# Moving a mixed block to third place and a whole product to the end: the late stage of an attention and MLP-mixer kernel

## The chip, the cores and the metric

The kernel runs on one core of one Trainium2 chip. A core has several engines that run at the same time, each through its own list of instructions in order: TensorE (PE) multiplies matrices into PSUM banks, VectorE (DVE), ScalarE (ACT) and GpSimd (POOL) work element by element, SyncE (SP) issues transfers (DMAs). An engine waits on semaphores that others raise. The metric is device time in microseconds (us) of one execution; three runs of the kernel before gave 1227.75, 1227.9 and 1229.17, median 1227.9.

## The reference

The inputs are q, k, v of shape (8, 8, 576, 64) (batch, head, token, feature), a scalar tau, and four weights. All is float32.

```python
scores = scale * np.matmul(q, k.transpose(0, 1, 3, 2))
thresh = np.max(scores, axis=-1, keepdims=True) - tau
scores = np.where(scores >= thresh, scores, -1000000000.0)
attn = softmax(scores)                       # written out in the reference
x = np.matmul(attn, v)                       # then (B,H,S,D) -> (B, S, H*D)
h = np.maximum(x^T @ w_tok1, 0.0) @ w_tok2   # over tokens, 576 -> 256 -> 576
u = x + h^T
h2 = np.maximum(u @ w_ch1, 0.0) @ w_ch2      # over channels, 512 -> 1536 -> 512
return u + h2
```

The last two lines are what this document is about: for each of the 8 x 576 tokens, u has 512 channels, the hidden layer 1536.

## The kernel before

**The planner.** The kernel is a Python program that writes out the instruction lists. For most of the work it makes operations (`sched.op`) with an engine, an assumed cost, the operations they depend on and a rank; a list scheduler then walks a clock of assumed times and emits them one after another, so that each engine's order is fixed when the program is built. Semaphore waits follow from the data, not from the assumed times. An operation on TensorE that needs a PSUM bank is made by `put_bank`, one that goes on in the same bank by `put_more`; `put_mid` reads a bank, and `put_leave` reads it and gives it back.

**The early stage** (to about 864 us) does attention batch by batch, the token products, and the channel products of a part of the tokens. What is put off: of batches 1 to 6 the second 256 tokens, of batch 7 all, and of every batch the last 64 tokens (576 is 256 + 256 + 64). Put-off values of batches 0 to 6 lie in DRAM (`spill`), those of batch 7 in SBUF (`xTs[7]`).

**The late stage** takes what was put off in five blocks of 512 tokens (class `Late`; the list is `groups`, made at L1377 to L1381). Before, they are: batches 1 and 2, batches 3 and 4, batches 5 and 6, batch 7's first 512 tokens, and last the "rests", 64 tokens from each of the 8 batches. A block's values are loaded into one of two buffers `u` (`load`, one DMA per batch; L1447 in the profile); batch 7's own block needs no load. The output rows are stored in four quarters of 128 rows (`store`, L1455), one DMA per batch in the quarter: a block of two batches, or of batch 7, has four stores of 128 rows, the rests have eight of 64 rows.

**A block.** Channels and tokens are each cut into two halves of 256, and a product of 2 x 2 such blocks is made with seven products in place of eight (Strassen's method in Winograd's form), with sums and differences on VectorE. `make_first` does the first layer in six rounds. Meanwhile VectorE transposes u in 32 x 32 blocks (`turn_u`, L1483, into `us`), and 16 DMAs per block bring the pieces into place (`move_u`, L1490, from `us` to `ut`), since the output is token by channel and has u added to it.

**The second layer** (`make_second`) is done for two halves m = 0, 1, each with 128 + 128 tokens (t = 0, 1) and 256 + 256 channels (n = 0, 1). Write o(t, n) for a piece of the output in `us` and old(t, n) for the same piece of u in `ut`. Three of its seven products, x1, x2 and x5, are whole ones (`plain`, six matrix multiplications of 128 x 256). The other four, x4, x6, x7 and x3, are split again into seven small products each of three multiplications of 128 x 128 (`make_inner`, called with 0 to 3). The whole product x5 is of `sum_place(0, m)` with `w2s[:, 0]`; it belongs into o(1, 1) and o(0, 1). Before, `y5b` adds it to old(0, 1) and `y5` puts it with old(1, 1) into o(1, 1). The last steps are sums: `q00`, `q01a`, `q01b`, `u2`, `u3`, `q10a`, `q10b`, `q11`, on POOL or VectorE as the planner finds; of these `q11` adds `w7` (which then holds u3) to o(1, 1), and `q01b` adds u2 (`w6_place`) to o(0, 1). The stores follow: the quarter t = 1 needs `q10b` and `q11`, the quarter t = 0 needs `q00` and `q01b`.

In the profile all late products have the line L1430 (`multiply`), all sums L946 (`add`) and differences L949 (`sub`), so they are told apart by tile names: `ga` and `hidden_b` hold the hidden layer, `x_sb`, `late_a` and `late_x` lend their space for sums, `small_a` and parts of the former two hold the small products' intermediate sums, `w` stands for several weights and for `w7`.

Of the kernel before, what the change touches and what calls it, by code (L numbers as in the profile page):

```python
# [21 lines left out]
def kernel(  # L22
# [25 lines left out]
    nc = tc.nc  # L48
    B, H, S, D = q.shape
# [15 lines left out]
    GR = 2 * P  # L65
# [29 lines left out]
    HJ, HD = NJ // 2, DM // 2  # L95
    w2s = const.tile([P, 3, HJ, HD], F32, name="w2s")
# [630 lines left out]
    sched = Scheduler()  # L727
# [217 lines left out]
    def add(out, a, b, eng=None):  # L945
        (eng or nc.vector).tensor_tensor(out=out, in0=a, in1=b, op=ALU.add)  # L946

    def sub(out, a, b, eng=None):
        (eng or nc.vector).tensor_tensor(out=out, in0=a, in1=b, op=ALU.subtract)  # L949
# [390 lines left out]
    def home(what):  # L1340
        if what not in homes:
            homes["g"] = work.tile([P, HJ, 2 * GR], F32, tag="g", bufs=1, name="ga")
            homes["a"] = work.tile([P, NTK, DM], F32, tag="a", bufs=1, name="late_a").rearrange("p m x -> p (m x)")
            homes["xT"] = work.tile([P, NP, S], F32, tag="xT", name="late_x").rearrange("p c x -> p (c x)")
        return homes[what]
# [4 lines left out]
    def sum_place(kind, m):  # L1350
        i = 2 * kind + m
        at = flat[:, TILE * i : TILE * i + TILE] if i < 3 else home("a")[:, 0:TILE]
        return at.rearrange("p (j x) -> p j x", x=P)
# [23 lines left out]
    REST = S - 2 * GR  # L1377
    put_off = [(b, GR * i, GR) for b in range(B) for i in range(NOW[b], 2)]
    groups = [put_off[i : i + 2] for i in range(0, len(put_off), 2)]
    assert all(len(g) == 2 for g in groups) and not NOW[B - 1]  # L1380
    groups.append([(b, 2 * GR, REST) for b in range(B)])  # L1381

    pending = [x for x in sched.ops if x.end is None and x.row is not None]
    last = [x for x in pending if x.row < B - 1]
# [27 lines left out]
    def put_bank(cost, work, deps, rank):  # L1412
        x = sched.op("pe", cost, work, deps, rank)
        x.bank = True
        return x
# [4 lines left out]
    def put_mid(on, cost, fn, x, deps, rank=1):  # L1420
        return sched.op(on, cost, lambda: fn(x.bank[1]), deps, rank)

    def put_leave(on, cost, fn, x, deps, rank=1):
        y = sched.op(on, cost, fn, deps, rank)
        y.frees = x
        return y

    def multiply(to, pairs, start=True):
        for x, (l, r) in enumerate(pairs):
            nc.tensor.matmul(to, lhsT=l, rhs=r, start=start and x == 0, stop=x == len(pairs) - 1, skip_group_check=not start)  # L1430

    small_used = [[], []]

    class Late:
# [12 lines left out]
                nc.sync.dma_start(out=self.u[:, :, at : at + n], in_=src)  # L1447
                at += n

        def store(self, t, rows):  # L1450
            at = 0
            for b, lo, n in groups[self.n]:
                first, last = max(at, P * t), min(at + n, P * t + P)
                if first < last:
                    nc.sync.dma_start(  # L1455
                        out=out[b, lo + first - at : lo + last - at, :], in_=rows[first - P * t : last - P * t]
                    )
                at += n
# [115 lines left out]
        def make_second(self, hidden, moved):  # L1574

            def a(i, k, m):
                return (hidden_b if k else home("g"))[:, :, GR * i + P * m : GR * i + P * m + P]

            def o(t, n, m):
                return self.us[m][:, t].rearrange("q a x -> q (a x)")[:, HD * n : HD * n + HD]  # L1580

            def old(t, n, m):
                return self.ut[m][:, t].rearrange("q k (c d) -> q c k d", c=NCC)[:, HC * n : HC * n + HC]

            def four(x):
                return x[:, 0:HD].rearrange("q (c k d) -> q c k d", c=HC, k=4)

            self.second, self.stores, self.outs = [], [[], []], [[], []]
            past_sums = list(self.past_second)
            h11, h12, h2 = hidden["11"], hidden["12"], hidden["2"]  # L1590

            def plain(l, r, deps):
                x = put_bank(2.57, lambda bank: multiply(bank[:, 0:HD], [(l()[:, j, :], r()[:, j, :]) for j in range(HJ)]), deps, 3.6 + 2 * self.n)
                self.second.append(x)
                return x

            def on_pool(fn, deps, rank=3):
                return sched.op("pool", 0.85, lambda: fn(nc.gpsimd), deps, rank, other=("dve", 0.36, lambda: fn(nc.vector)))

            s1, s2, s3, s4, y2, x2 = ([None, None] for _ in range(6))  # L1600
            for m in range(2):
                s1[m] = sched.op("dve", 0.96, lambda m=m: add(sum_place(0, m), a(1, 0, m), a(1, 1, m)), h12 + h2 + past_sums, 2)
            for m in range(2):
                s2[m] = sched.op("dve", 0.96, lambda m=m: sub(sum_place(1, m), sum_place(0, m), a(0, 0, m)), [s1[m]] + h11 + past_sums, 2)
                s3[m] = sched.op("dve", 0.96, lambda m=m: sub(a(1, 0, m), a(0, 0, m), a(1, 0, m)), [s1[m]] + h11, 2)
            c1, y5, y5b = [None, None], [None, None], [None, None]
            x1 = []
            for m in range(2):
                x2[m] = plain(lambda m=m: a(0, 1, m), lambda: side2(1, 0), h2)
                y2[m] = put_leave("dve", 0.42, lambda bank, m=m: add(four(o(0, 0, m)), four(bank), old(0, 0, m)), x2[m], [x2[m]] + moved[m])  # L1610
                x1.append(plain(lambda m=m: a(0, 0, m), lambda: side2(0, 0), h11))
                c1[m] = put_leave("act", 0.37, lambda bank, m=m: nc.scalar.copy(out=p1_place(m), in_=bank[:, 0:HD]), x1[m], [x1[m]] + past_sums, 0)
                s4[m] = sched.op("dve", 0.96, lambda m=m: sub(a(0, 1, m), a(0, 1, m), sum_place(1, m)), [s2[m], x2[m]], 2)
            for m in range(2):
                x5 = plain(lambda m=m: sum_place(0, m), lambda: w2s[:, 0], [s1[m]])
                y5b[m] = put_mid("dve", 0.42, lambda bank, m=m: add(old(0, 1, m), four(bank), old(0, 1, m)), x5, [x5] + moved[m])
                y5[m] = put_leave("dve", 0.42, lambda bank, m=m: add(four(o(1, 1, m)), four(bank), old(1, 1, m)), x5, [x5, y5b[m]] + moved[m])
            w7_of = lambda m: w7[:, m, :]
            w4 = self.make_inner(0, lambda m: a(1, 1, m), lambda m: o(1, 0, m), [h2, h2], s1, [moved[0], moved[1]])
            w6 = self.make_inner(1, lambda m: sum_place(1, m), w6_place, [[s2[0]], [s2[1]]], s4, [past_sums, past_sums])  # L1620
            w7s = self.make_inner(2, lambda m: a(1, 0, m), w7_of, [[s3[0]], [s3[1]]], [], [past_sums, past_sums])
            w3 = self.make_inner(3, lambda m: a(0, 1, m), lambda m: o(0, 1, m), [[s4[0]], [s4[1]]], x2, [moved[0], moved[1]])
            all_second = []
            for m in range(2):
                q00 = on_pool(lambda eng, m=m: add(o(0, 0, m), o(0, 0, m), p1_place(m), eng), [y2[m], c1[m]])
                u2 = on_pool(lambda eng, m=m: add(w6_place(m), w6_place(m), p1_place(m), eng), w6[m] + [c1[m]], rank=2)
                q01a = on_pool(lambda eng, m=m: add(four(o(0, 1, m)), four(o(0, 1, m)), old(0, 1, m), eng), w3[m] + [y5b[m]])
                q01b = on_pool(lambda eng, m=m: add(o(0, 1, m), o(0, 1, m), w6_place(m), eng), [q01a, u2])
                u3 = on_pool(lambda eng, m=m: add(w7_of(m), w7_of(m), w6_place(m), eng), w7s[m] + [u2], rank=2)
                q10a = on_pool(lambda eng, m=m: add(four(o(1, 0, m)), four(o(1, 0, m)), old(1, 0, m), eng), w4[m])  # L1630
                q10b = on_pool(lambda eng, m=m: add(o(1, 0, m), o(1, 0, m), w7_of(m), eng), [q10a, u3])
                q11 = on_pool(lambda eng, m=m: add(o(1, 1, m), o(1, 1, m), w7_of(m), eng), [y5[m], u3])
                self.outs[m] = [q00, q01b, q10b, q11]
                for t, deps in ((1, [q10b, q11]), (0, [q00, q01b])):
                    count = 2 if len(groups[self.n]) > 2 else 1
                    self.stores[m].append(
                        sched.op("sp", 0.6, lambda m=m, t=t: self.store(2 * t + m, self.us[m][:, t].rearrange("q a x -> q (a x)")), deps, 1, dmas=(count, 256 // count, 0.6))
                    )
                all_second += self.outs[m]
            self.past_next = all_second + self.second  # L1640

# [95 lines left out]
```

## Time and profile before

| what | us |
|---|---|
| median of three runs | 1227.9 |
| the profiled execution's own time | 1229.42 |
| its span, first to last instruction | 1227.6 |
| first stores of the five late blocks issued at | 938.74, 1009.29, 1079.85, 1150.42, 1218.01 |
| TensorE's last product begins and ends | 1219.02, 1219.93 |
| last instruction on VectorE ends | 1222.26 |
| mean granted TensorE clock | 0.997 |

In the profile, a row of a timeline gives start, length, engine, line, operation, "output<-inputs", shape, the number of merged instructions and, in brackets, the idle time before it and who ended it. SPq is SyncE's queue of transfers. One multiplication of this float32 kernel is two rows on TensorE. Rows of TensorE overlap, so the pitch from start to start says more than the length. PEld is the load of weights beside the products.

### The profile page before, as it was taken

To read this page: it belongs to the slowest core of one execution; us is meant where nothing else is said; L and a number is where in the kernel's file an instruction comes from. 1 tells how busy PE (TensorE), PEld (TensorE's weight loads), DVE (VectorE), ACT (ScalarE), POOL (GpSimd) and SP (SyncE) were. 2 spreads that over 40 slices of the span, in tenths; PEclk is the share of its full clock that TensorE was granted. 3 is DMA by queue.
4 is the path that set the end of the run, shared out by engine and by line. 5 is a ranking of instruction groups with operands and counts; after the bars stand their busy time and mean duration, and the time that the engine had idled before them with its cause. 6 is when DMAs were issued, how large, how long until landed. Compare 5 with 4: busy or idle time off the path is not lost.

```text
span 1227.6 us, 21546 instructions
## 1 busy us (share of the span) xinstructions
PE 1199.0 (98%) x7769; PEld 972.6 (79%) x7769; DVE 877.8 (71%) x1406; ACT 572.6 (47%) x1279; POOL 365.7 (30%) x568
## 2 busy tenths in 40 slices
PE   9888999999999999999999999999999999999996
PEld 8655788777777777876877777788899898999986
DVE  6798996777778668776867766843767575766756
ACT  6987863555663665574555456530211212121220
POOL 3666552333343423332433323411001010110101
PEclk9999999999999999999999999999999999999999
DMA  8656867767778757877767687661211202020101
GB/s 145 140 121 163 234 169 169 153 145 179 175 161 185 174 124 178 182 158 168 161 153 168 151 183 152 151 165 34 52 35 47 58 18 53 1 69 1 54 17 35
DMA packets 325370, 149.76 MB, mean 122 GB/s; under 512 B 223824, under 2 KB 318032, under 8 KB 325264
## 3 DMA queue, kind: packets, MB, share of 16 engines
q1 hardware_dynamic: 323392, 148.17, 52.9%
q8 instruction: 62, 1.02, 0.3%
q10 hardware_dynamic: 1872, 0.21, 0.1%
q14 instruction: 44, 0.36, 0.1%
HBM read 47.32 MB, written 13.50 MB: 50 GB/s over the span
## 4 chain that ended last, share of the span: by engine, by line
PE 85%; DVE 2%; DMA 0%; ACT 0%; issue 0%; SPq 0%; DVEq 0%
PE bank L1430 28%; PE bank L1058 12%; PE bank L982 11%; PE sc L848 10%; PE bank L371 8%; PE bank L460 5%; PE bank L478 5%; PE bank L366 3%; PE bank L1073 2%; DVE mx L865 1%; PE bank L441 0%; DVE us L946 0%; DVE g L1066 0%; DMA lk<-in_k_dram 0%; ACT e L881 0%
## 5 line engine op out<-in xcount | busy, mean ns | idle before, releaser
L881 ACT ACTIVATE e<-sc,bias 128x576 f32<-128x576 f32 x288 | 194.3, 742 | 173.1 <-POOL bias L871 171.9
L286 POOL TENSOR_SCALAR e<-e,rr 128x576 f32<-128x576 f32 x288 | 216.6, 769 | 189.3 <-DVE rr L278 187.8
L891 ACT ACTIVATE e<-e,ntau 128x576 f32<-128x576 f32 x288 | 220.8, 780 | 0.2
L865 DVE TENSOR_REDUCE mx<-sc 128x2 f32<-128x1152 f32 x144 | 188.1, 1348 | 40.5 <-PE sc L848 39.8
L316 DVE STREAM_TRANSPOSE T<-e 128x1152 f32<-128x1152 f32 x126 | 171.0, 1365 | 31.0 <-POOL e L286 21.8
L1058 PE MATMUL bank<-xT,wc 128*128 128x256 f32 x768 | 177.1, 383 | 1.9 <-ACT g L1063 0.9
L848 PE MATMUL sc<-kT,qT 64*128 64x192 f32 (+1 forms) x1920 | 165.5, 333 | 1.0 <-ACT e L881 1.0
L1058 PEld LDWEIGHTS bank<-xT,wc 128*128 128x128 f32 x768 | 143.0, 190 | 28.9 <-issue 4.4
L848 PEld LDWEIGHTS sc<-kT,qT 64*128 64x128 f32 (+1 forms) x1920 | 138.4, 176 | 31.2 <-issue 19.3
L371 PE MATMUL bank<-eT,lv 128*64 128x384 f32 (+1 forms) x1024 | 135.1, 406 | 0.0
L371 PEld LDWEIGHTS bank<-eT,lv 128*64 128x64 f32 x1024 | 73.7, 137 | 50.5 <-issue 44.3
L871 POOL TENSOR_SCALAR bias<-mx,toff 128x2 f32<-128x2 f32 x144 | 39.3, 273 | 193.1 <-DVE mx L865 186.0
L946 POOL TENSOR_TENSOR us<-us,late_x 128x256 f32<-128x256 f32 x14 | 13.1, 934 | 219.9 <-DVE us L946 156.9
L982 PE MATMUL bank<-wc,g 128*128 128x256 f32 x336 | 77.8, 381 | 0.0
L478 PE MATMUL bank<-w,a 128*128 128x192 f32 (+1 forms) x256 | 74.4, 425 | 1.2 <-DVE xT L489 0.7
L460 PE MATMUL bank<-x_sb,w 128*128 128x256 f32 x320 | 73.0, 383 | 0.7 <-DVE x_sb L445 0.5
L982 PEld LDWEIGHTS bank<-wc,g 128*128 128x128 f32 x336 | 63.1, 190 | 12.8 <-issue 2.5
L460 PEld LDWEIGHTS bank<-x_sb,w 128*128 128x128 f32 x320 | 59.8, 190 | 10.9 <-issue 1.1
L478 PEld LDWEIGHTS bank<-w,a 128*128 128x128 f32 x256 | 43.6, 192 | 22.5 <-issue 6.4
L1430 PE MATMUL bank<-t,w1s 128*128 128x256 f32 x240 | 60.8, 379 | 0.0
L946 DVE TENSOR_TENSOR temps<-bank,temps 128x256 f32<-128x256 f32 x60 | 25.3, 422 | 49.5 <-PE bank L1430 47.1
L1430 PE MATMUL bank<-t,wc 128*128 128x256 f32 x240 | 59.2, 379 | 0.0
(175 smaller groups left out, 1820.0 us busy)
## 6 DMA issues: line engine op xcount, KB each, us to landing
eT<-T SPq DMA_DIRECT2D x504, 144.0 KB, 3.0
w2s<-in_moe_w_ch_dram SPq DMA_DIRECT2D x24, 512.0 KB, 4.2
lk<-in_k_dram SPq DMA_DIRECT2D x122, 72.0 KB, 2.9
ut<-us SPq DMA_DIRECT2D x136, 64.0 KB, 2.1
lq<-in_q_dram SPq DMA_DIRECT2D x120, 72.0 KB, 3.1
out_dram<-us SPq DMA_DIRECT2D x32, 256.0 KB, 2.1
lv<-in_v_dram SPq DMA_DIRECT2D x112, 72.0 KB, 2.5
spill<-xT SPq DMA_DIRECT2D x6, 640.0 KB, 4.0
```

Of the source, the lines that this page charges most:

```text
L286: nc.gpsimd.tensor_scalar(out=eh, in0=eh, scalar1=rr[:, h : h + 1], scalar2=1.0, op0=ALU.mult, op1=ALU.mult)
L316: nc.vector.transpose(out=T.rearrange("p a (c x) -> p c a x", c=NK), in_=e.rearrange("p (c a x) -> p c a x", c=NK, a=4))
L371: nc.tensor.matmul(to[r], lhsT=lv[:, j, :], rhs=e[j], start=False, stop=(c == NI - 1), skip_group_check=True)
L460: nc.tensor.matmul(to, lhsT=w1[:, t, P * m : P * m + P], rhs=x(t), start=(t == 0), stop=(t == NT - 1), skip_group_check=len(products) > 1,)
L478: nc.tensor.matmul(bank[:, n * i : n * i + n], lhsT=hidden[b][:, m, P * c : P * c + P], rhs=w2[:, m, lo : lo + n], start=(m == 0), stop=(m ...
L848: nc.tensor.matmul(sc[h][rows, f, HT * k : HT * k + HT], lhsT=qT[r, cols], rhs=kT[r, HT * f : HT * f + HT], start=True, stop=True, skip_gr ...
L865: nc.vector.tensor_reduce(out=mx[:, h], in_=sc[h][:, :, 0 : 2 * HT].rearrange("p f (k x) -> p k f x", k=2), axis=AX.XY, op=ALU.max)
L881: nc.scalar.activation(out=eh, in_=part[h], func=AF.Prelu, bias=bias[:, h], scale=SCALE, alpha=STEEP)
L891: nc.scalar.activation(out=eh, in_=eh, func=AF.Exp, bias=ntau, accum_out=rs[:, h, 0:1])
L982: nc.tensor.matmul(bank[:, 0:HD], lhsT=x[:, j, :], rhs=y[:, j, :], start=j == 0, stop=j == HJ - 1)
L1058: nc.tensor.matmul(bank[:, 0:n], lhsT=wc1[:, j, c, :], rhs=uT[:, c, GR * i : GR * i + n], start=(c == 0), stop=(c == NCC - 1))
L1430: nc.tensor.matmul(to, lhsT=l, rhs=r, start=start and x == 0, stop=x == len(pairs) - 1, skip_group_check=not start)
```

## The change

The list of blocks has the rests third in place of last, so batch 7's own 512 tokens come last. In the block that is last (`ends`), x5 is not made early: u3 is added to old(1, 1) (`b11`, in place); x5 depends in the planner on the sums of the small products, so it comes late; `q11` is then the bank plus old(1, 1) into o(1, 1), and a second step adds the bank to o(0, 1) and gives the bank back. The stores of the quarters t = 1 of that block are issued by ACT, those of t = 0 by SP. In every block `q01a` names the moves of u among its dependencies.

```diff
-    groups.append([(b, 2 * GR, REST) for b in range(B)])
+    groups.insert(2, [(b, 2 * GR, REST) for b in range(B)])
...
-        def store(self, t, rows):
+        def store(self, t, rows, eng=None):
...
-                    nc.sync.dma_start(
+                    (eng or nc.sync).dma_start(
...
-            for m in range(2):
+            ends = self.n == len(groups) - 1
+            for m in range(0 if ends else 2):
                 x5 = plain(lambda m=m: sum_place(0, m), lambda: w2s[:, 0], [s1[m]])
                 y5b[m] = put_mid(...)
                 y5[m] = put_leave(...)
...
-                q01a = on_pool(..., w3[m] + [y5b[m]])
+                q01a = on_pool(..., w3[m] + [y5b[m]] + moved[m])
...
-                q11 = on_pool(lambda eng, m=m: add(o(1, 1, m), o(1, 1, m), w7_of(m), eng), [y5[m], u3])
+                if ends:
+                    b11 = on_pool(lambda eng, m=m: add(old(1, 1, m), old(1, 1, m), four(w7_of(m)), eng), [u3] + moved[m])
+                    x5 = plain(lambda m=m: sum_place(0, m), lambda: w2s[:, 0], [s1[m]] + small_used[0] + small_used[1][:1])
+                    q11 = put_mid("dve", 0.42, lambda bank, m=m: add(four(o(1, 1, m)), four(bank), old(1, 1, m)), x5, [x5, b11])
+                    q01b = put_leave("dve", 0.42, lambda bank, m=m: add(o(0, 1, m), bank[:, 0:HD], o(0, 1, m)), x5, [x5, q11, q01b])
+                else:
+                    q11 = on_pool(lambda eng, m=m: add(o(1, 1, m), o(1, 1, m), w7_of(m), eng), [y5[m], u3])
...
-                    self.stores[m].append(
-                        sched.op("sp", 0.6, lambda m=m, t=t: self.store(2 * t + m, ...), deps, 1, dmas=(count, 256 // count, 0.6))
-                    )
+                    rows = lambda m=m, t=t: self.us[m][:, t].rearrange("q a x -> q (a x)")
+                    if ends and t:
+                        x = sched.op("act", 0.53, lambda m=m, t=t, rows=rows: self.store(2 * t + m, rows(), nc.scalar), deps, 1)
+                    else:
+                        x = sched.op("sp", 0.6, lambda m=m, t=t, rows=rows: self.store(2 * t + m, rows()), deps, 1, dmas=(count, 256 // count, 0.6))
+                    self.stores[m].append(x)
```

More of the change, by code (lines that the diff above doesn't have):

```diff
@@ L1626, in make_second @@
                 u2 = on_pool(lambda eng, m=m: add(w6_place(m), w6_place(m), p1_place(m), eng), w6[m] + [c1[m]], rank=2)
-                q01a = on_pool(lambda eng, m=m: add(four(o(0, 1, m)), four(o(0, 1, m)), old(0, 1, m), eng), w3[m] + [y5b[m]])
+                q01a = on_pool(lambda eng, m=m: add(four(o(0, 1, m)), four(o(0, 1, m)), old(0, 1, m), eng), w3[m] + [y5b[m]] + moved[m])
                 q01b = on_pool(lambda eng, m=m: add(o(0, 1, m), o(0, 1, m), w6_place(m), eng), [q01a, u2])
@@ L1635, in make_second @@
                     count = 2 if len(groups[self.n]) > 2 else 1
-                    self.stores[m].append(
-                        sched.op("sp", 0.6, lambda m=m, t=t: self.store(2 * t + m, self.us[m][:, t].rearrange("q a x -> q (a x)")), deps, 1, dmas=(count, 256 // count, 0.6))
-                    )
+                    rows = lambda m=m, t=t: self.us[m][:, t].rearrange("q a x -> q (a x)")
[4 more added lines that the diff above has]
+                    self.stores[m].append(x)
                 all_second += self.outs[m]
```

## The prediction

> **What bounds the kernel now.** I read the page's busy shares first, then the waits of TensorE over the late blocks, then the timeline of the last 30 us engine by engine, then the same stretch cut into windows.
>
> ```profile
> span 1227.6 us, 21546 instructions
> ...
> PE 1199.0 (98%) x7769; PEld 972.6 (79%) x7769; DVE 877.8 (71%) x1406; ACT 572.6 (47%) x1279; POOL 365.7 (30%) x568
> ```
> ```profile
> PE bank L1430 <- DVE us L946: 2.0, 2, 1.6
> ```
>
> The second fence is the whole answer to "what did TensorE wait for from 880 to 1228 us": two waits, 2.0 us. Through five late blocks TensorE has no hole until the end of the last one. So a change here can only win at the end, and can lose wherever it opens a hole.
>
> ```profile
> 1202.45 2.75 PE L1430 MATMUL bank<-w2s,x_sb 128*128 128x256 f32 x12
> 1205.05 0.83 PE L1430 MATMUL bank<-inner,hidden_b 128*128 128x128 f32 x6
> ...
> 1206.91 0.94 PE L1430 MATMUL bank<-w2s,hidden_b 128*128 128x128 f32 x6 [0.36 <-DVE us L946]
> 1207.76 0.94 PE L1430 MATMUL bank<-w2s,x_sb 128*128 128x128 f32 x6
> 1208.53 0.83 PE L1430 MATMUL bank<-w,ga 128*128 128x128 f32 x6
> 1209.20 0.83 PE L1430 MATMUL bank<-wc,ga 128*128 128x128 f32 x6
> ...
> 1216.57 0.83 PE L1430 MATMUL bank<-wc,ga 128*128 128x128 f32 x6
> 1219.02 0.91 PE L1430 MATMUL bank<-wc,hidden_b 128*128 128x128 f32 x6 [1.61 <-DVE us L946]
> ```
> ```profile
> 1218.59 0.28 DVE L946 TENSOR_TENSOR us<-bank,late_a 128x128 f32<-128x128 f32 x1
> 1218.79 0.56 DVE L946 TENSOR_TENSOR w<-w,late_x 128x256 f32<-128x256 f32 x1
> 1219.38 1.70 DVE L946 TENSOR_TENSOR us<-us,w 128x256 f32<-128x256 f32 x2
> 1220.99 0.28 DVE L946 TENSOR_TENSOR us<-bank,x_sb 128x128 f32<-128x128 f32 x1
> 1221.38 0.43 DVE L946 TENSOR_TENSOR us<-us,ut 128x256 f32<-128x256 f32 x1
> 1221.84 0.42 DVE L946 TENSOR_TENSOR us<-us,late_x 128x256 f32<-128x256 f32 x1
> ```
> ```profile
> 1150.42 4.37 SPq L1455 DMA_DIRECT2D out_dram<-us  x4
> ...
> 1218.01 6.79 SPq L1455 DMA_DIRECT2D out_dram<-us  x8
> ```
>
> See in the first of these the pitch of TensorE: a whole product (12 rows) takes 1205.05 - 1202.45 = 2.60 us, a small one 0.67 (1208.53 to 1209.20). See the gap before the last product: its slot was 1216.57 + 0.67 = 1217.24, it ran at 1219.02, 1.78 lost, because VectorE freed its bank only at 1218.87. Then see VectorE working on until 1222.26 with TensorE finished at 1219.93, and the stores last: six of the eight go out from 1221.14 to 1224.80, 0.61 apart. So after TensorE's last product 7.67 us pass (1219.93 to 1227.6): VectorE, then the queue of 64-row stores, then about 1.0 us from the last landing (issued 1224.2, landing 2.4) to the end.
>
> **The change part by part.** Every instruction of all five engines stands in the same order as before, except where told here; TensorE does the same products, VectorE the same number of operations.
>
> *The whole products x5 of the last block move behind the others.* Before, they cover VectorE's work at 1197.19 and 1202.45. Without them the seven small products behind 1197.19 follow at 0.67: x5 of the first and x7, x5, x6 and so on at 1197.19, 1197.86, 1198.53, 1199.20, 1199.87, 1200.54. Is VectorE in time? Its operand for the one at 1199.20 is 0.56 long and starts when the product of 1197.19 ends (row length 0.83): 1198.63, in time. The one for 1200.54 starts at 1199.41, ends 1199.97, in time. For the next (slot 1201.21) it needs two sums of 0.30 and one of 0.29 after 1200.53: 1201.44, so 0.28 us of hole, then 0.16 at its sister, against 0.53 and 0.18 before (1206.91 against 1205.71 + 0.67; 0.85 against 0.67). The product of 1208.53 starts at 1203.2: 5.3 us earlier, 5.2 being the two products and 0.1 the holes. The bounds: 0.4 less if no hole is left, 2.8 more if each of the two becomes the longest one in the trace (1.6). I take the worked value, since the row lengths are those of the same operations.
>
> *The last small product loses its hole.* From 1203.2 all follows 5.3 earlier, with VectorE, which is then in the same order up to the operations above. The first whole product starts in the slot 1217.24 - 5.3 = 1211.9 and ends at 1214.5; there the last small product goes, whose bank is free at 1218.87 - 5.3 = 1213.6: no wait, 1.78 us won. The second whole product runs 1215.2 to 1217.9 (row length 2.75).
>
> *VectorE behind it.* The pair at 1219.38, slowed to 0.85 each beside POOL's rows of 0.79, ends at 1215.8; the sum for half a block from its whole product 0.42, then rows of 0.28, 0.43, 0.42 and the second sum 0.42 end at 1217.8. So VectorE is free 0.1 before the last product ends: nearly a tie. Then two sums from the bank, 0.42 long at a pitch of 0.34 (as the pair after the whole product at 1202.45): 1217.95 to 1218.7. Bounds of these two: 0.42 each as every row from a bank is, or 0.85 as the pair beside POOL; POOL's last row ends at 1220.8 - 5.3 = 1215.5, so I take 0.42. The Trainium skill ("SBUF — State Buffer", Who interferes with whom) says that an operation with at most one SBUF input does not contend with GpSimd, and one with two does; by it the two sums would stay at 0.42 even with POOL busy, and the sum would not change; without it they could end 0.9 later, at a time of 1223.3. The trace agrees so far: the row from a bank at 1218.59 kept its 0.28 beside POOL's 0.46 at 1218.61, and the pair of SBUF inputs behind it did not keep its 0.38.
>
> *The stores.* The last block is batch 7's own 512 tokens, so four stores of 128 rows in place of eight of 64. The last goes out at 1218.8 on SP, its neighbour at 1218.4 on ACT, the one before at 1217.8. Stores of 128 rows land in 2.0 us each at 1150 (median) and 2.9 at the longest of all stores. In the DMA view by slices their data take 0.8 us at 330 to 410 GB/s, those of 64 rows run at about 205. Three of 0.8 from 1218.6 on end at 1221.0, so I take a landing of 2.3 (1221.1), and the 1.0 us behind it: 1222.1. No store from ACT is in these rows; its first loads at the start of the trace take 0.5 us each to issue, against 0.34 to 0.6 on SP. ACT has nothing behind it, so bounds are those of the landing, -0.3 and +0.6. The Trainium skill ("DMA: Bandwidth & Descriptors", Issuing engines are not separate DMA queues) says that a second issuing engine saves only issue time, the transfers sharing the same engines. By it the ACT queue is worth the 0.3 us of an issue, which is what the sum has; if the queues were separate, the last would land 0.3 earlier. No run so far shows two queues storing at once.
>
> *The block of rests as third.* Load: eight pieces in place of two at 903.35; eight took 6.0 us at 973.91 and land in 3.2, so by 913, and its first sum on VectorE is at 974.26; SP's next work is at 938.74. Nothing. The fourth block's load becomes short and waits for the same buffer. Stores: eight at 1079.85 in place of four over 4.36. VectorE's first transpose of the next block (1085.16) waits for the first four; the second pair is ready when POOL's row ends at 1081.5, goes at 1081.6 and 1082.2, and lands by 1084.6 (2.4) or 1085.1 (2.9). Queued behind that transpose is the sum that releases TensorE's bank, which had 1.13 us of idle time. The other four go at 1082.8 to 1084.6, land by 1087.5, and are needed at 1089.33. SP's moves behind them start at 1086.31. Cost 0, at the worst 0.1. If the cover were gone, TensorE would starve of banks microsecond for microsecond.
>
> *Sum.* TensorE's end: 1219.9 - 5.3 (two products and 0.1 of holes fewer ahead) + 5.2 (the two now at the end) - 1.8 (hole) - 0.1 (row ends) = 1217.9. Behind it 7.7 becomes 0.8 + 0.1 + 2.3 + 1.0 = 4.2. Span 1222.1, 5.5 us less. The profiled execution took 1229.4, of which 1.8 lie outside the span; with 5.5 less it would be 1223.9. Against the median 1227.9, 1.5 below it, the forecast is 1222.4.
>
> **The rivals.**
>
> Cover missed (R1): both holes behind 1201 grow to 1.6, +2.7, 1225.1. For it: VectorE is at 0.83 of its time from 1207.8 on. Against: the operands counted above are early by 0.5 us each.
>
> Stores keep the end (R2): three whole stores run at the 205 GB/s of the present end, 786 KB in 3.8 us from 1218.6, then 1.5 as now from last data (1226.1) to end: span 1224.0, time 1224.3. Against it the 128-row rows at 1150.
>
> Slower (R3): in the middle, at the fourth block's transposes (1085.16 and 1089.33), which wait in VectorE's order for the stores of the rests. If 64-row stores came one after another at 2.4 us each, the eighth would land at 1099, 9.8 late; less 1.1 idle, 8.7 lost: 1231.1. It decides from 9.1 late on (5.5 gained, 2.5 beyond). Against: six such stores leave 0.61 apart at the end of this trace, and land in 2.3 to 2.4.
>
> No change (R4): the end is set by something that neither list shows, and the product's sums only move the stores' wait: about 1227.
>
> **How the numbers follow.** My sum 0.70, R1 0.10, R2 0.12, R3 0.04, R4 0.04. 0.2% (2.5 us, about what a measurement here can tell) puts the line at 1225.4; a fifth of R1 falls beyond it: faster 0.90, same 0.06, slower 0.04. The range goes down by the landing (0.3), the holes (0.4), the part of the 1.0 at the end that SP spent waiting for TensorE's queue (0.6 by the waits) and the runs' own spread below their median (0.2) to 1220.9, and up to R1's 1225.1; what is left out is R3, R4 and little more.
>
> **What would show it.** Right: one TensorE wait at most around 1201, the last two whole products back to back with one small product between, ending near 1217.9; last VectorE row from a bank ending at 1218.7; four stores of 256 KB, two of them ACT's. R2 would show in their landing (over 3 us), R1 in TensorE's waits for VectorE before 1205, R3 in a hole near 1085 to 1100. The prediction is wrong if VectorE still has more than 1.5 us of rows behind the last product.

## The result and the profile after

| | median, us | runs |
|---|---|---|
| before | 1227.88 | 6, 1227.57 to 1230.0 |
| after | 1223.99 | 6, 1223.12 to 1226.3 |

The ratio is 0.9967, with a 95% interval of 0.9954 to 0.998: 3.9 us less, between 2.5 and 5.6. The changed kernel is faster, by 0.3%. The prediction said 1222.4, in a range of 1220.9 to 1225.1.

First the page of the changed kernel: its span, the busy time of each engine, and the packets of a queue that is new to the late stage, ACT's.

```profile
span 1221.9 us, 21551 instructions
...
PE 1197.8 (98%) x7769; PEld 971.3 (79%) x7769; DVE 877.7 (72%) x1406; ACT 572.9 (47%) x1279; POOL 366.0 (30%) x568
...
q10 hardware_dynamic: 2160, 0.74, 0.2%
```

TensorE's and VectorE's work is what it was (1199.0 and 877.8 us before), in as many instructions. So nothing was saved in work; what went is time in which engines waited. The profiled execution took 1223.68 us and its span is 5.7 us shorter than before's.

Next the timeline of its last 25 us: TensorE, then VectorE's last three rows, then the two queues that issue the stores.

```profile
1199.92 0.83 PE L1430 MATMUL bank<-w,late_a 128*128 128x128 f32 x6
1200.84 0.94 PE L1430 MATMUL bank<-w2s,hidden_b 128*128 128x128 f32 x6
1201.79 0.94 PE L1430 MATMUL bank<-w2s,x_sb 128*128 128x128 f32 x6
1202.56 0.83 PE L1430 MATMUL bank<-w,ga 128*128 128x128 f32 x6
...
1210.60 0.83 PE L1430 MATMUL bank<-wc,ga 128*128 128x128 f32 x6
1211.27 2.76 PE L1430 MATMUL bank<-w2s,x_sb 128*128 128x256 f32 x12
1213.86 0.83 PE L1430 MATMUL bank<-wc,hidden_b 128*128 128x128 f32 x6
1214.53 2.76 PE L1430 MATMUL bank<-w2s,x_sb 128*128 128x256 f32 x12
...
1215.67 2.52 ACTq L1455 DMA_DIRECT2D out_dram<-us  x2
...
1216.86 0.42 DVE L946 TENSOR_TENSOR us<-bank,us 128x256 f32<-128x256 f32 x1
1217.32 0.43 DVE L946 TENSOR_TENSOR us<-bank,ut 128x256 f32<-128x256 f32 x1
1217.42 1.02 SPq L1455 DMA_DIRECT2D out_dram<-us  x2
1217.66 0.41 DVE L946 TENSOR_TENSOR us<-bank,us 128x256 f32<-128x256 f32 x1
```

See the whole products x5 at 1211.27 and 1214.53, with the last small product between them at the pitch of 2.59 and 0.67 that full work has: the hole of 1.78 us is gone. TensorE's waits from 880 us to the end, two of 2.0 us before, are an empty list in this execution. Two holes too short for that list are left, 0.25 us before 1200.84 and 0.28 before 1201.79, read from the pitch. And after TensorE's end at 1217.29 only two sums of VectorE follow, to 1218.07.

Last the transfers of 1214 to 1222 us, cut into slices of 0.2 us; the rows below give the size of a store and its median time from issue to landing.

```profile
GB/s 0 0 0 0 0 0 0 0 0 0 0 0 82 420 369 379 62 0 0 0 0 236 379 399 369 379 420 369 359 420 369 236 0 0 0 0 0 0 0 0
...
out_dram<-us ACTq DMA_DIRECT2D x2, 256.0 KB, 2.2
out_dram<-us SPq DMA_DIRECT2D x2, 256.0 KB, 2.4
```

The first store flows from 1216.4 to 1217.4, the other three back to back from 1218.2 to 1220.4. Their last data lie 1.5 us before the end of the span. Before, eight stores of 64 rows flowed until 1226.2 in a span of 1227.6, the last stretch of them at about 205 GB/s.

**A ruler that leaves the early stage out.** Executions of one kernel differ by microseconds in the attention stage (more on this at the end), so traces are compared from a point that all of them share: the first of the small products that the page names `bank<-w,late_a`, in the last block. "Stretch" is from its start to the end of the span; it is cut at the end of VectorE's last row into the work and the tail. All runs of this study stand here.

| kernel | that product starts | to VectorE's end | tail | stretch | span |
|---|---|---|---|---|---|
| before | 1195.85 | 26.41 | 5.34 | 31.75 | 1227.6 |
| after | 1195.23 | 22.84 | 3.83 | 26.67 | 1221.9 |
| e0_after, the changed kernel again | 1194.35 | 22.84 | 3.81 | 26.65 | 1221.0 |
| e1_order, only the new order of blocks | 1198.89 | 26.40 | 3.31 | 29.71 | 1228.6 |
| e2_product, only x5 and the two queues | 1198.22 | 22.84 | 5.04 | 27.88 | 1226.1 |
| e3_sp, all stores from SP | 1195.57 | 22.83 | 3.80 | 26.63 | 1222.2 |
| e4_pieces, the rests' stores in 16 | 1195.48 | 22.84 | 3.78 | 26.62 | 1222.1 |
| e5_halves, last stores cut by channels | 1196.16 | 22.86 | 2.78 | 25.64 | 1221.8 |
| e6_two_queues, last stores of 64 rows, two queues | 1194.99 | 22.84 | 4.67 | 27.51 | 1222.5 |
| e7_one_queue, the same stores, one queue | 1193.47 | 22.84 | 5.79 | 28.63 | 1222.1 |

The work repeats to 0.03 us in every kernel that has the same products, over three chips, so hundredths can be read here where the medians can't tell a microsecond. The change takes 5.08 us from the stretch: 3.57 of work and 1.51 of tail. The other 0.62 us of the profiled difference came before it.

### The profile page after: what moved, and what is told of

The parts are those of the page before. It is cut to its first block, busy times and chain, and to the rows that moved or that the text cites. A ratio compares the mean times of both kernels' runs of the same rounds, so it can differ in the third digit from the quotient of the medians.

```text
span 1221.9 us, 21551 instructions
## 1 busy us (share of the span) xinstructions
PE 1197.8 (98%) x7769; PEld 971.3 (79%) x7769; DVE 877.7 (72%) x1406; ACT 572.9 (47%) x1279; POOL 366.0 (30%) x568
## 4 chain that ended last, share of the span: by engine, by line
PE 86%; DVE 1%; ACT 0%; issue 0%; DVEq 0%
PE bank L1430 29%; PE bank L1058 13%; PE bank L982 11%; PE sc L848 10%; PE bank L371 9%; PE bank L460 5%; PE bank L478 5%; PE bank L366 3%; PE bank L1073 2%; DVE mx L865 0%; PE bank L441 0%; ACT e L881 0%; DVE g L1066 0%; PE bank L1071 0%; DVE us L946 0%; DVE g L946 0%
```

## The experiments

### The changed kernel again, and its two halves

Theory: two parts act. The order of the blocks turns eight stores of 64 rows at the end into four of 128 rows, which shortens the tail; the moved product fills TensorE's hole and takes work from behind TensorE's end. Rival R2: stores keep the end whatever the products do. Rival R3: the order costs something in the middle. The first run is the changed kernel itself, beside the others on the same chip.

> The changed kernel once more, for a tighter number. My sum (the gain is all at the end, 5.1 to 5.5 us of span, and the rest of the program is as long as before): 1227.9 - 5.1 to 5.5 = 1222.4 to 1222.8 at the median. The rival reading of the first six runs (their medians are only 3.9 us apart, so about 1.3 us are lost again somewhere outside the last block or outside the span): 1224.0. The trace parts them: by my sum the stretch from the first small product of the pair with late_a (1195.85 before) to the end of the span is 31.75 us before and 26.7 here, and the first stores of the late blocks keep their spacing of 70.5 us; by the rival one of those spacings is longer, or the time outside the span is over 2.2.

Measured: 1223.56 against 1229.1 before, ratio 0.9953 (0.9938 to 0.9969), a stretch of 26.65. The median lies above the 1222.4 to 1222.8 of the sum, but so does the kernel before beside it lie above its 1227.9: the difference, 5.5, is at the upper end of the 5.1 to 5.5 that was expected. The rival's signs are absent: the first stores of the first four late blocks are 70.4 to 70.7 us apart, and 1.9 us of this execution lie outside its span.

Only the order:

```diff
 # in the kernel before
-    groups.append([(b, 2 * GR, REST) for b in range(B)])
+    groups.insert(2, [(b, 2 * GR, REST) for b in range(B)])
```

> The kernel before with the rests third, and nothing else changed: the whole products stay early, all stores leave from SP. My sum: TensorE's hole of 1.6 to 1.8 us before the last small product stays, VectorE still ends 2.3 us behind TensorE, and only the stores get shorter: the last one goes out when VectorE ends (1222.3 on the clock of before) in place of 1224.2 and lands in 2.0 to 2.3 in place of 2.4, so 1.9 to 2.3 us less: 1225.6 to 1226.0. Rival (the order is worth nothing by itself, the stores of 64 rows were not the end): 1227.9. Rival (the rests in the middle cost TensorE time): over 1228, with a wait of TensorE between 1084 and 1100.

Measured: 1227.22, ratio 0.9984 (0.9972 to 0.9996), which is 1.9 less than the 1229.1 beside it; the stretch 2.04 shorter. Its waits of TensorE, and the rows of its end:

```profile
PE bank L1430 <- DVE us L946: 2.0, 2, 1.6
```
```profile
1222.05 0.91 PE L1430 MATMUL bank<-wc,hidden_b 128*128 128x128 f32 x6 [1.60 <-DVE us L946]
...
1224.87 0.42 DVE L946 TENSOR_TENSOR us<-us,late_x 128x256 f32<-128x256 f32 x1
...
1221.05 4.64 SPq L1455 DMA_DIRECT2D out_dram<-us  x4
```

TensorE's hole of 1.6 is there as before, VectorE ends 26.40 after the common point as before (26.41), and only the tail fell, from 5.34 to 3.31. So the order alone is worth 2.03 us, all of it in the stores.

Only the product (and the queues): the rests stay last.

```diff
 # in the changed kernel
-    groups.insert(2, [(b, 2 * GR, REST) for b in range(B)])
+    groups.append([(b, 2 * GR, REST) for b in range(B)])
```

> The changed kernel with the rests last as before: the whole products late, the stores of eight times 64 rows from two queues. My sum: TensorE and VectorE end as in the changed kernel (1217.9 and 1218.7 on the clock of before), but the six last stores of 64 rows run at about 205 GB/s: 786 KB from 1217.0 or 1218.6 on are 3.8 us, then 1.5: end of the span 1223.0 to 1224.0, 3.6 to 4.6 us less than before: 1223.3 to 1224.3 at the median, and 1.0 to 1.9 more than the changed kernel. Rival (two queues double the rate of 64-row stores): end as in the changed kernel, 1222.4 to 1222.8, with over 300 GB/s in the last slices.

Measured: 1225.17, ratio 0.9962 (0.995 to 0.9973); on before's clock the span would end at 1195.85 + 27.88 = 1223.73, inside what was expected. VectorE ends 3.57 earlier, as in the changed kernel, but the tail keeps 5.04 of 5.34. Its end, and its transfers from 1218 to 1226 in slices of 0.2 us:

```profile
1218.65 3.30 ACTq L1455 DMA_DIRECT2D out_dram<-us  x4
1220.40 2.78 SPq L1455 DMA_DIRECT2D out_dram<-us  x4
1220.65 0.41 DVE L946 TENSOR_TENSOR us<-bank,us 128x256 f32<-128x256 f32 x1
```
```profile
GB/s 0 0 0 0 0 0 0 0 0 174 266 174 164 205 266 62 0 0 215 225 184 195 195 184 164 379 389 266 184 338 359 430 195 31 0 0 0 0 0 0
```

Stores of 64 rows flow at 160 to 270 GB/s at first, but at 340 to 430 in several slices near the end, after both queues had stores waiting. So the constant 205 of my sum is only half right, and the rival has its fast slices but not its early end; e6 and e7 take this up.

The halves together would be 2.04 + 3.87 = 5.91; the change has 5.08. The difference, 0.83, is in the tail: the order takes 2.03 from it alone and the product 0.30, both together 1.51. With the order alone and with the whole change, the last three stores flow in a row for 2.2 us. With the order alone the first two of them are issued 1.1 and 0.7 us before VectorE ends, with the product at the end 0.65 and 0.23, so more of the 2.2 us lies behind VectorE's end. The 3.87 of the product has the second queue in it: the rests last, the product late and one queue was not run, and e6 and e7 below put a second queue at 1.12 us for stores of 64 rows.

### The second queue

```diff
-                    if ends and t:
+                    if False:
                         x = sched.op("act", 0.53, ...)
```

> The changed kernel with all four last stores from SP. My sum: the second queue saves one issue at most, 0.0 to 0.4 us more than the changed kernel, below what the times can tell; in the trace the last store is issued at most 0.3 later behind VectorE's last row, and the last landing is within 0.4. Rival (separate queues carry more together): the three last stores of 256 KB need 0.8 each one after another and the end comes 0.8 or more later.

Measured: 1223.94, ratio 0.9958 (0.9943 to 0.9974), a stretch of 26.63 against 26.67 and 26.65. The transfers from 1214 to 1222:

```profile
GB/s 0 0 0 0 0 0 0 0 0 0 0 0 0 0 225 399 389 287 10 0 0 0 41 338 369 420 359 358 430 369 359 420 369 103 0 0 0 0 0 0
```

The same picture with one queue: once the three last stores are ready, their data run at 340 to 430 GB/s without a break. The 256 KB of a store flow for 0.7 us and the issue of the next takes 0.34, so a second issuer has nothing to save. The two queues of the change are worth 0.0 us. The Trainium skill ("DMA: Bandwidth & Descriptors", Issuing engines are not separate DMA queues) has the transfers share the same engines, and this run of 128-row stores agrees; for stores of 64 rows a second queue was worth more than the time of issuing (e6 and e7 below).

### Is there room in the middle?

R3 was that the eight stores of the rests, now in the middle, make the next block's transposes late. In the first trace of the changed kernel no transpose waits for them. In e0's trace, of the same kernel, the first one does:

```profile
1084.30 1.11 DVE L1483 STREAM_TRANSPOSE us<-u 128x512 f32<-128x512 f32 x1 [0.56 <-DMA out_dram<-us]
1085.91 0.42 DVE L946 TENSOR_TENSOR ga<-bank,temps 128x256 f32<-128x256 f32 x1 [0.50 <-PE bank L1430]
```

It waits 0.56 us for the stores, and the sum behind it still waits 0.50 for TensorE, so nothing is lost. In e3, e5 and e7 the same transpose waits 0.21, 0.20 and 0.15. To see whether there is a margin or luck, their stores were cut into 16 of 32 rows.

```diff
-                if first < last:
+                step = 32 if len(groups[self.n]) > 2 else P
+                for f in range(first, last, step):
+                    l = min(f + step, last)
                     (eng or nc.sync).dma_start(
-                        out=out[b, lo + first - at : lo + last - at, :], in_=rows[first - P * t : last - P * t]
+                        out=out[b, lo + f - at : lo + l - at, :], in_=rows[f - P * t : l - P * t]
```

> The changed kernel with the rests' stores cut into sixteen pieces of 32 rows in place of eight of 64; the order on all engines is that of the changed kernel. It asks how much room the rests have in the middle. In the changed kernel the eight take 5.96 us from 1079.40 on, VectorE's two transposes come at 1084.68 and 1088.72, and TensorE waits nowhere. My sum (no cost because the stores land just in time): sixteen pieces 0.6 apart leave over 9.7 us; the first eight land by 1086.7, 2.0 behind 1084.68, the others by 1091.5, 2.8 behind 1088.72; VectorE has 1.0 and 0.4 us of idle time behind these transposes, so it falls 1.0 to 2.4 us behind and TensorE shows waits for VectorE of 0.5 to 2.5 us in all between 1085 and 1098. Rival (there is ample room, eight banks and the other engines cover it): no wait of TensorE from 880 us on, and the spacing of the late blocks stays at 70.5 us.

Measured: 1224.18 in one run, a stretch of 26.62. The changed kernel's SP and VectorE around it:

```profile
1079.40 5.96 SPq L1455 DMA_DIRECT2D out_dram<-us  x8
1085.82 12.69 SPq L1490 DMA_DIRECT2D ut<-us  x16
...
1084.68 1.12 DVE L1483 STREAM_TRANSPOSE us<-u 128x512 f32<-128x512 f32 x1
1088.72 1.11 DVE L1483 STREAM_TRANSPOSE us<-u 128x512 f32<-128x512 f32 x1
```

and this kernel's:

```profile
1079.49 8.04 SPq L1457 DMA_DIRECT2D out_dram<-us  x16
...
1085.47 1.11 DVE L1485 STREAM_TRANSPOSE us<-u 128x512 f32<-128x512 f32 x1 [0.59 <-DMA out_dram<-us]
1087.04 0.42 DVE L946 TENSOR_TENSOR ga<-bank,temps 128x256 f32<-128x256 f32 x1 [0.47 <-PE bank L1430]
```

My sum for this kernel, 0.5 to 2.5 us of TensorE waits, fell. It had put the 16 issues at some 0.6 us apart; they came 0.5 apart and landed in 1.7. VectorE's transpose did wait 0.59 us for the stores, the wait that R3 named, but VectorE made it up: the sum behind it waited 0.47 for TensorE's bank, so it was still early. TensorE waits for nothing from 880 us on. The wait is hardly longer than the 0.56 that eight stores gave in e0. The move to third place costs nothing, and in this one run it cost nothing with the store issue 2.1 us longer either; the 0.47 is an estimate of the room that is left.

### What the last tail is made of

With the three last stores of 128 rows, 512 channels, the last store is issued at 1218.11 and lands 2.8 us later, since it flows behind the other two. If that queue is the tail, bytes should leave earlier. In e5 the last block's stores are cut by channels: a quarter of the output (128 rows) goes in two stores of 256 channels, each as soon as its own half is summed, so half of the bytes leave before the last products end.

```diff
+                if ends:
+                    for t, n, dep in ((0, 0, q00), (1, 0, q10b), (1, 1, q11), (0, 1, q01b)):
+                        def put_half(t=t, n=n, m=m, rows=rows):
+                            self.store(2 * t + m, rows(t), nc.scalar if t else nc.sync, slice(HD * n, HD * n + HD))
+                        ...                      # "act" for t = 1, "sp" for t = 0
```

> The changed kernel with each of the last block's four stores cut by columns into two of 128 rows x 256 channels (128 KB), of which four can leave before the whole products end. It asks whether the end is set by the bytes that are still to go, or by the fixed way from an issue to the end, and is the version that might beat both. In the changed kernel the last three stores (786 KB at 380 GB/s, 2.1 us) keep the last one waiting: it lands in 2.8 us, where a lone one lands in 2.0. My sum: only 393 KB go after the last whole product, so the last lands in 2.0 to 2.2, 0.6 to 0.8 us earlier: the stretch from the first small product with late_a to the end is 25.9 to 26.1 us against 26.67; the median 0.7 below the changed kernel's, too little for the times to tell. Rival (128 KB pieces are slow however they are cut, as the rests' were): the last four run at about 205 GB/s, 524 KB in 2.6 us, and the stretch is 27 us or more.

Measured: 1222.93 against 1229.3, ratio 0.9947 (0.9933 to 0.9961); a stretch of 25.64, 1.03 less than the changed kernel's where 0.6 to 0.8 was expected. Stores issued from 1218 on, and the transfers from 1214 to 1222:

```profile
out_dram<-us SPq DMA_DIRECT2D x2, 128.0 KB, 1.8
out_dram<-us ACTq DMA_DIRECT2D x1, 128.0 KB, 1.8
```
```profile
GB/s 5 0 0 0 0 0 0 0 0 0 179 364 113 0 0 0 0 200 353 103 0 0 0 0 0 102 343 236 292 359 348 277 10 0 0 0 0 0 0 0
```

The work is the same (22.86), the last landing 1.8 in place of 2.8, the tail 2.78 in place of 3.83: all of the gain is the earlier landing of the last store. How much of it is the shorter queue in front and how much its own half size, this run doesn't part. By the trace this version beats both kernels. By the medians it isn't told apart from the changed kernel, which was timed on another chip: the interval of its ratio, 0.9933 to 0.9961, overlaps e0's.

### Rows or queues

e2 left open why stores of 64 rows ran at about 205 GB/s and then at 400. In e6 and e7 the last block's stores are cut into rows 0 to 63 and rows 64 to 127 of each quarter; e6 sends the first half from SP and the second from ACT, e7 sends both from SP.

```diff
-                if first < last:
+                if self.own and first < last:
+                    for h, e in enumerate((nc.sync, nc.scalar)):      # e7: (nc.sync, nc.sync)
+                        f = first + 64 * h
+                        e.dma_start(out=out[b, lo + f - at : lo + f + 64 - at, :], in_=rows[f - P * t : f + 64 - P * t])
+                elif first < last:
```

> The changed kernel with each of the last block's four stores of 128 rows cut into rows 0 to 63 from SP and rows 64 to 127 from ACT (eight stores of 64 rows, on two queues at once). With the next run it measures what two queues are worth to stores of 64 rows. In the run with the rests last and the whole products late, the slices showed 160 to 225 GB/s while one queue was busy, and 340 to 430 GB/s once both had a store under way. Theory A (a store of 64 rows reaches only half of the way into memory, and two queues fill both halves): the last three pairs run at 340 to 430 GB/s, and the stretch from the first small product with late_a to the end is 26.4 to 26.9 us, as in the changed kernel (26.67). Theory B (a second queue saves issue time only, and the transfers share one rate): about 205 GB/s to the end, and a stretch of 28 us or more.

> The same eight stores of 64 rows, all from SP. Both theories: about 205 GB/s, stores 0.6 us apart, as at the end of the kernel before; the last one is issued about 1.8 us after VectorE's last row less what the earlier ones leave room for, and the stretch from the first small product with late_a to the end is 27.5 to 28.5 us. If it came out under 27.0, the width of a store would be worth nothing and the shorter stretch of the kernel with the rests third would have another cause.

Measured: 1224.37 and 1224.01 in one run each, against 1230.54 in one of before; stretches of 27.51 (e6) and 28.63 (e7). The transfers of e6, then of e7, from 1214 to 1222:

```profile
GB/s 0 0 0 0 0 0 0 0 0 0 0 0 0 174 205 174 164 410 185 0 0 113 215 174 256 369 410 399 123 348 348 338 246 410 144 41 0 0 0 0
```
```profile
GB/s 0 0 0 0 0 92 236 195 205 215 195 164 10 51 225 195 164 246 215 184 195 205 225 174 215 195 205 215 205 164 287 174 164 31 0 0 0 0 0 0
```

From one queue the 64-row stores keep to about 200 GB/s to the end, and e7 came out 0.13 above its range. The issue isn't what holds them back: from 1216.7 to 1220.8 their packets fill 87.5% of the time of the 16 DMA engines. Over the 8 us they take 59.1% of it, against 35.0% for the same bytes in stores of 128 rows (e3), so the packets, 2 KB in both, take longer. With two queues the last six stores flow for 2.9 us (1218.2 to 1221.1) in place of 4.0 in e7 (1216.8 to 1220.8). That is the 1.12 by which the stretch of e6 is shorter. The same bytes in three stores of 128 rows took 2.2 in the changed kernel.

Theory A's mechanism, two halves flowing side by side, is not what the trace shows. Several of its fast slices come almost wholly from one queue. These rows have the packets, MB and packet time of SP's queue (q1) and ACT's (q10), the last as a share of the 16 engines' time, which can come out over 100% in a short window: e6 from 1217.4 to 1217.6 at 410 GB/s, then e2 from 1224.1 to 1224.4 at 396.

```profile
q1 hardware_dynamic: 40, 0.08, 105.0%
q10 hardware_dynamic: 9, 0.00, 2.5%
...
q1 hardware_dynamic: 74, 0.12, 114.2%
```

In the first, ACT's store of rows 64 to 127 had flowed before, alone and at 184 GB/s (1216.6 to 1217.2), and SP's of rows 0 to 63 followed, nearly alone, at 410. So a store of 64 rows can flow at the full rate with no other beside it. e2 hints that the half counts and not the queue: by the order of issue, ACT's third store follows one of the same half and flows at 176 GB/s (1222.3 to 1223.0), and SP's next, of the other half, at 384 together with the rest of ACT's (1223.0 to 1223.4). No run tests that by itself, and why a store should gain from what flowed before it stays open.

The stretch of e6 lies between its two expectations, 0.84 behind the changed kernel. R2 is answered all the same: at the end of the changed kernel the rate is that of 128-row stores, not 205.

## Why the prediction was right

The times of the changed trace stand here with 0.62 us added, since its last block began 0.62 earlier than before's (1195.23 against 1195.85), which is the early stage's doing.

| step of the prediction | put at | measured |
|---|---|---|
| the two holes, without x5 as cover, together | 0.44 | 0.53 |
| the product of 1208.53 starts | 1203.2 | 1203.18 |
| first whole product x5 starts | 1211.9 | 1211.89 |
| last small product starts, no wait | 1214.5 | 1214.48 |
| second whole product, start and end | 1215.2, 1217.9 | 1215.15, 1217.91 |
| VectorE's last row ends | 1218.7 | 1218.69 |
| last store issued | 1218.8 | 1218.73 |
| its landing | 2.3 | 2.8 |
| from landing to the end of the span | 1.0 | 1.0 |
| span ends | 1222.1 | 1222.52 |

**The cover and the hole.** Right: the two holes are 0.09 us longer than worked out, and R1 (both holes at 1.6) did not come. That the product of 1208.53 starts at the forecast time to 0.02 is partly luck: by the prediction's own rows the holes shrink from 0.71 to 0.44, by 0.27 and not by the 0.1 that its sum has, so the sum should have read about 1203.1, and the longer holes made up for most of the slip. The hole of 1.78 went whole. e2 shows 3.57 us of work gone with the rests still last, so it is the product that does it and not the order.

**VectorE behind TensorE.** Right, and narrow as said: VectorE's previous row ends at 1217.28, TensorE at 1217.29. The last two sums take 0.42 and 0.41. POOL's last row is over at 1214.83, so this trace can't show what they would take beside POOL.

**The stores.** The mechanism was right, one term was mis-sized. The prediction let three stores flow until 1221.0; measured, 1220.4 + 0.62 = 1221.0, as they started 0.2 later and took 0.73 each in place of 0.8. But it let the last one land 0.1 us after its last data, and it took 0.5 (issued 1218.11 + 2.8 = 1220.9, data until 1220.4). Before's own trace had the number: the prediction's R2 reads 1.5 us from last data to the end there, where its main sum uses 0.1 + 1.0. With 1.5 in both, the sum gives 1222.5, which is what came. The 0.3 us for ACT's queue was wrong as well: e3 has 0.0.

**The rests third.** Right at 0. The wait of the transposes does come, 0.56 us in e0, and the idle time behind it covers it, as the prediction had it; e4 shows the same with a longer row of stores.

**The time.** Here the size was off most: 5.5 us were taken from the median and 3.9 measured, though the trace says 5.08 for the late stage. The repeat gave 5.5 (3.8 to 7.6), the first measurement 3.9 (2.5 to 5.6); both intervals hold 5.1. The kernel before moved more than the changed one: its median was 1227.9 over 6 executions, but 1229.1 over 22 and 1229.3 over 11 beside the experiments, while the changed one gave 1224.0 and 1223.6. In the traces, what moves is the stage that the change leaves alone. The first store of the late stage, which lies before everything that the change moves, went out at 938.74 before and 938.28 after, but anywhere from 936.36 (e7) to 941.95 (e1):

```profile
937.23 4.36 SPq L1455 DMA_DIRECT2D out_dram<-us  x4
```
```profile
941.95 4.36 SPq L1455 DMA_DIRECT2D out_dram<-us  x4
```

These are e0's and e1's, 4.7 us apart. In the windows of the two (length, busy time of PE, PEld, DVE, ACT and POOL, then the granted TensorE clock, the DMA share and GB/s), the stretch of 100 to 300 us differs in the clock:

```profile
100.00:300.00 200.00, 195.19 (x1371) 150.56 (x1370) 162.10 (x232) 122.02 (x265) 85.52 (x121) 1.00 0.72 171
```
```profile
100.00:300.00 200.00, 194.93 (x1350) 149.17 (x1351) 158.44 (x230) 121.75 (x264) 85.90 (x120) 0.98 0.72 170
```

e0 was granted 1.00 there and finished 1371 rows of products, e1 0.98 and 1350. The other executions go the same way: of the 33 of the kernel before that stand beside the experiments, the seven with a mean granted clock of 0.995 or less have spans of 1228.6 to 1231.6 us, the eleven with 0.998 have 1225.5 to 1228.3. That the clock is the cause of the whole spread is argued from this, not shown by an experiment.

## What to carry to other kernels

Keep for the very end the product whose results need the fewest steps afterwards: its length covers the other engine's sums, and only its own sums lie behind it. Let the last stores run over 128 rows each and send early what is ready early, so that few bytes queue in front of the last store; put a block of awkward stores in the middle, where an order with slack hides them. And when a gain of a few microseconds at one end is judged, measure from a point inside the trace that both kernels share.

## What the runs showed of the hardware

- Stores of 128 rows flowed at 340 to 430 GB/s, stores of 64 rows from one queue at about 205 (e7), in packets of the same size. The Trainium skill ("SBUF — State Buffer", Door 1: The DMA port swizzle) lets 64 partitions reach half of the ports; a row of a store is a partition here, and the rates of single queues agree in kind.
- With two queues, six stores of 64 rows flowed for 2.9 us in place of 4.0 (e6 and e7). The queues took turns in part, and a store that followed one of the other half flowed nearly alone at about 400 GB/s; why is open.
- A second issuing queue was worth 0.0 us for stores of 256 KB (e3), and 1.12 us for stores of 64 rows (28.63 - 27.51, e7 to e6).
- The time to landing doesn't follow the bytes alone: 64 KB (32 rows) took 1.7 us, issued 0.5 us apart (e4); 128 KB as 128 rows of 256 channels 1.8 (e5); 256 KB as 128 rows 2.0 (the stores at 1150 before) and 2.8 as the third of three in a row; 128 KB as 64 rows 2.3 (e7) to 2.8 (e6, SP).
- At the end of a kernel some 1.3 to 1.5 us lie between the last data of a store and the end of the span; in the changed kernel 1.5, 0.5 of them to its landing.
